# VectorE's order in the steady part written by hand, and one tensor-engine visit a tile for the local jobs

## The chip, the cores and the metric

The kernel runs on one core of a Trainium2 chip. The metric is the device time of one execution in microseconds (us). Five engines matter here, each with its own queue: TensorE (PE; its weight loads are PEld), VectorE (DVE), ScalarE (ACT), GpSimd (POOL) and SyncE (SP), which issues the DMAs.

## The reference

An attention layer feeds a feed-forward layer. There are 8 batches, 8 heads, 576 tokens and 64 channels a head; the feed-forward layer goes from 512 to 2048 and back to 512.

```python
scores = scale * q @ k.T                              # a head at a time
mask_local   = (rel >= 0) & (rel < 32)                # heads 0 to 3
mask_strided = (rel >= 0) & (pos_k % 32 == pos_q % 32)  # heads 4 to 7
attn = softmax(where(mask, scores, -1e9))
x = (attn @ v).transpose(0, 2, 1, 3).reshape(4608, 512)
h = x @ w_in                                          # 512 -> 2048
out = gelu(h) @ w_out                                 # 2048 -> 512
```

All of it is float32.

## The kernel before

**Tiles and steps.** The 4608 tokens make 12 tiles of 384 (`NTILE`, `TT`). The 2048 hidden channels make 16 chunks of 128 (`NF`), so the feed-forward layer has 192 steps; step n belongs to tile n // 16 and chunk n % 16, and `ready[t] = 16 t` is the first step of tile t. Every float32 operand is held as a high part and the difference to it, and a product is three matmuls. In a step, `ffn_h(n)` makes 12 matmuls (L602 to L604) into one of two PSUM banks with the tag H; `ffn_g(n)` lets ScalarE apply gelu in place (L611) and copy the high part gh (L613), and VectorE make the difference gl (L615); `ffn_o(n - 2)` makes 9 matmuls (L641 to L643) into three output banks. `store` copies a finished tile out.

**Attention.** The first four heads are local. A local job (`band_job`, 3 a tile, `JPT`) covers 128 tokens and yields between its parts: (0) score matmuls, L290, into the banks S0 and S1; (1) VectorE takes the masked minimum, L304; (2) ScalarE's exp, L308; (3) VectorE normalises and transposes, L311 to L314, and SyncE copies eight blocks into a band; (4) value matmuls, L328; (5) ScalarE's high part of x, L230; (6) VectorE's difference, L232. The other four heads are strided and run on VectorE alone but for their exp. A unit of up to 4 rows has `strided_qk`: a fill of the scores by GpSimd, one product-and-sum for each pair of rows (L477), a maximum and its subtraction (L485, L486); then `strided_av`: sum, reciprocal and quotient (L503 to L507), one multiply-add for each pair (L517, L519), and a transpose (L527, `fin`), which puts a `split` on a list: ScalarE's high part and VectorE's difference into the tile of x.

**Order.** The first 16 steps (`NB`) and the attention of the first two tiles are an order written out by hand (`START`), for all engines. The steady part is a loop over `step(n)`. Inside `tc.manual_schedule(engines=...)` the named engines run their instructions in the order in which the program issues them; the others are ordered by a scheduler, which may put a later instruction ahead of one that it believes is not ready. Before the change TensorE and ScalarE are named in the steady part, and VectorE, GpSimd and SyncE are scheduled.

**What a step issues, before.** `visit(n)`: at step 2 of a tile the score matmuls of the three local jobs of the next tile (`score_at`), at step 12 their value matmuls (`value_at`). Then H, gelu, gh and gl of step n; the high parts and differences of splits made earlier; `softmaxes(n)`, which issues parts 5, 6, 1, 2 and 3 of the local jobs; ScalarE's strided exps (`flush_exps`); a share of the strided list (`run_strided`); and the O matmuls of step n - 2. The share is set by sums of estimated costs:

```python
need = last[c] + (last[c + 1] - last[c]) * min(1.0, max(0.0, (n - a + 1) / (e - a - 3)))
run_strided(max(need, tot * (n - N0) / (ready[-1] - 3 - N0)))
```

Here c is the tile, a and e its first step and the next tile's (a is one more in tile 0), `last[t]` the summed cost up to the last entry that tile t needs, `tot` all of it. The list goes unit by unit: the q-k part of unit u, then the value part of unit u - 1.

Of the kernel before, what the change touches and what calls it, by code (L numbers as in the profile page):

```python
# [23 lines left out]
P = 128  # L24
STRIDE = 32
TT = 384
LU = 64
# [55 lines left out]
def attn_ffn_kernel(ctx: ExitStack, tc: tile.TileContext, qk, vl, qka, va, qs, ks, vs, w, out):  # L83
# [36 lines left out]
    def rows(j):  # L120
        return slice(j * D, (j + 1) * D)
# [112 lines left out]
    def local_job(x, banks=None, dve=0, pn=-1):  # L234
# [35 lines left out]
        dst = [a[:, 0:N2, c0:c0 + P] for a in x_tile(t)]  # L270
        yield from to_x(*dst, xv)

    def band_job(x, bt, sx=None):

        QB = STRIDE
        i = x % JPT if sx is not None else 0
        sx = {} if sx is None else sx
        if i == 0:  # L280
            sx["s"] = [ps_a.tile([P, DM], F32, name=f"S{j}_L{x}", tag=f"S{j}") for j in range(2)]
        s = [t[:, i * P:(i + 1) * P] for t in sx["s"]]
        qv = jq[x][:, 0:2 * N2 * LU].rearrange("p (r a t) -> p r a t", r=N2, a=2)
        kv = jq.pop(x)[:, 2 * N2 * LU:].rearrange("p (r a t) -> p r a t", r=N2, a=2)
        head = [(h % 2, slice(h // 2 * 2 * QB, (h // 2 + 1) * 2 * QB)) for h in range(HL)]
        for h in range(0, HL, 2):
            for g in range(P // QB):
                a, b = divmod(g, 2)
                for j in range(2):
                    nc.tensor.matmul(s[j][g * QB:(g + 1) * QB, head[h][1]],  # L290
                                     qv[rows(j), h // 2, a, b * QB:(b + 1) * QB],
                                     kv[rows(j), h // 2, a, b * QB:(b + 2) * QB],
                                     start=True, stop=True, tile_position=(j * D, g * QB))
        yield
        p1 = lpool.tile([P, 4 * LK], F32, name=f"P_L{x}", tag="P", bufs=2)
        p2 = lpool.tile([P, DM], F32, name=f"PT_L{x}", tag="PT", bufs=2)
        pb, pt = p2[:, 0:DM // 2], p2[:, DM // 2:]
        pv = pb.rearrange("p (c h t) -> p c h t", c=2, h=HL)
        nm, ss, rs = small(f"L{x}")
        first_ = [a for a in range(2) if LPLACE[2 * x + a][1] == 0]  # L300
        msk = bmask[first_[0] if first_ else None]
        for h in range(HL):
            j, cs = head[h]
            nc.vector.tensor_tensor_reduce(p1[:, h * 2 * QB:(h + 1) * 2 * QB], s[j][:, cs], msk, -SC, 3.0e38,  # L304
                                           ALU.add, ALU.min, nm[:, h:h + 1])
        yield
        for h in range(HL):
            nc.scalar.activation(pv[:, :, h, :], p1[:, h * 2 * QB:(h + 1) * 2 * QB].rearrange(  # L308
                "p (c t) -> p c t", c=2), AF.Exp, bias=nm[:, h:h + 1], scale=-1.0, accum_out=ss[:, h:h + 1])
        yield  # L310
        nc.vector.tensor_scalar_add(ss, ss, 1e-9)  # L311
        nc.vector.reciprocal(rs, ss)
        nc.vector.tensor_tensor(pv, pv, rs.unsqueeze(1).unsqueeze(3).to_broadcast([P, 2, HL, QB]), ALU.mult)
        nc.vector.transpose(pt, pb)  # L314
        tv = pt.rearrange("p (c q) -> p c q", c=2)
        for g in range(P // QB):
            for c in range(2):
                kb = g % 2 + c
                nc.sync.dma_start(bt[kb * QB:(kb + 1) * QB, g, :], tv[g * QB:(g + 1) * QB, c, :])
        yield  # L320
        if i % 2 == 0:
            sx["x"] = ps_a.tile([P, DM], F32, name=f"X_L{x}", tag="X" if i == 0 else "S0")
        xv = sx["x"][:, i % 2 * N2 * P:(i % 2 + 1) * N2 * P].rearrange("p (r q) -> p r q", r=N2)
        bv = bt.rearrange("p (a b) (h q) -> p a b h q", a=2, h=HL)
        for r in range(N2):
            for a in range(2):
                for j in range(2):
                    nc.tensor.matmul(xv[rows(j), r, a * LU:(a + 1) * LU], jv[x][:, a, 2 * r + j, :],  # L328
                                     bv[:LK, a, :, 2 * r + j, :], start=True, stop=True)
        jv.pop(x)  # L330
        load_jv(x + 3)
        yield
        t, c0 = divmod(x * P, TT)
        dst = [d[:, 0:N2, c0:c0 + P] for d in x_tile(t)]
        yield from to_x(*dst, xv)


    ka = {}
# [120 lines left out]
    def flush_exps(u):  # L459
        while exps and exps[0][0] <= u:  # L460
            exps.pop(0)[1]()

    def strided_qk(u):
        vi, _, r0, nr, t, k = PLACE[u]
        W = r0 + nr
        ops = []

        def init():
            s = spool.tile([P, UR, NR], F32, name=f"sc_{u}", tag="sc", bufs=3)[:, 0:nr]
            nc.gpsimd.memset(s[:, :, 0:W], NEG)  # L470
            ss[u] = s
        ops.append((0.0, init))
        for c in range(W):
            for r in range(max(0, c - r0), nr):
                def f(r=r, c=c):
                    junk = spool.tile([P, D], F32, name=f"junk_{u}_{r}_{c}", tag="junk", bufs=4)
                    nc.vector.tensor_tensor_reduce(  # L477
                        junk, sq[vi, "q"][:, r0 + r, :], sq[vi, "k"][:, c, :], 1.0, 0.0,
                        ALU.mult, ALU.add, ss[u][:, r, c:c + 1])
                ops.append((0.137, f))  # L480

        def sm():
            s = ss[u][:, :, 0:W]
            m = spool.tile([P, UR], F32, name=f"m_{u}", tag="m")[:, 0:nr]
            nc.vector.tensor_reduce(m, s, AX.X, ALU.max)  # L485
            nc.vector.tensor_tensor(s, s, m.unsqueeze(2).to_broadcast([P, nr, W]), ALU.subtract)  # L486
            exps.append((u, lambda: nc.scalar.activation(s, s, AF.Exp, scale=SC)))  # L487
        ops.append((0.25, sm))
        return ops
# [163 lines left out]
    strided = []  # L653
    N0 = 17
    U0 = sum(x[4] <= NA for x in PLACE)
    for u in range(U0, NU + 1):
        for v, what, names in ((u, strided_qk, "qk"), (u - 1, strided_av, "v")):
            if U0 <= v < NU:
                vi, _, r0, nr, t, _ = PLACE[v]
                strided += [(t, c, f) for c, f in what(v)]  # L660
                if r0 + nr == VISITS[vi][2] and vi in last_of:
                    strided.append((t, 0.0, lambda g=last_of[vi], ns=names: [load_strided(g, nm) for nm in ns]))
# [105 lines left out]

    SCORES, VALUES = 2, 12
    score_at = {ready[t - 1] + SCORES: t for t in range(2, NTILE)}
    value_at = {ready[t - 1] + VALUES: t for t in range(2, NTILE)}
    banks = {}
    local = {}
    band = slot("band", [P, 4 * DM])
    nc.gpsimd.memset(band, 0.0)
    NBT = 3
# [2 lines left out]
    def part(x, *which):  # L781

        for p in which:
            if p == 0:
                local[x] = [band_job(x, bts[x % NBT], banks), 0]
            assert local[x][1] == p
            local[x][1] += 1
            if next(local[x][0], True) is not None:
                load_jq(x + 3)

    def visit(n):

        for at, p in ((score_at, 0), (value_at, 4)):
            for i in range(JPT if n in at else 0):
                part(at[n] * JPT + i, p)

    def softmaxes(n):

        for i in range(JPT if n in value_at else 0):
            part(value_at[n] * JPT + i, 5, 6)  # L800
        for i in range(JPT if n in score_at else 0):
            part(score_at[n] * JPT + i, 1)
        for i in range(JPT):
            for d, p in ((1, 2), (2, 3)):
                t = score_at.get(n - 2 * i - d)
                if t is not None:
                    if p == 2:
                        flush_exps(NU)
                    part(t * JPT + i, p)

    def step(n):

# [2 lines left out]
        visit(n)  # L815
        if NB <= n < NS:
            ffn_h(n)
            for _ in ffn_g(n):
                pass
        old = len(splits)  # L820
        while old and n >= xfree[splits[0][0]]:
            for _ in splits.pop(0)[1]():
                pass
            old -= 1
        softmaxes(n)
        flush_exps(NU)
        if c + 1 < NTILE:
            a, e = ready[c] + (1 if c == 0 else 0), ready[c + 1]
            need = last[c] + (last[c + 1] - last[c]) * min(1.0, max(0.0, (n - a + 1) / (e - a - 3)))
            run_strided(max(need, tot * (n - N0) / (ready[-1] - 3 - N0)))  # L830
        if n == NS + 1:
            ffn_o(n - 3, n - 2)
        elif n >= NB + 2 and n < NS:
# [1 line left out]
        if n >= NB + 2 and (n - 2) % NF == NF - 1:  # L835
            store((n - 2) // NF)

    with tc.manual_schedule(engines={ET.Activation, ET.PE}):
        for n in range(NB, NS + 1):
            step(n)  # L840
    with tc.manual_schedule(engines={ET.Activation, ET.PE}):
        step(NS + 1)


# [63 lines left out]
```

## Time and profile before

| what | value |
| --- | --- |
| median of 3 runs | 885.21 us (884.99 to 885.87) |
| the profiled execution's own time | 885.1 us |
| its span in the profile | 883.2 us |
| TensorE clock granted, mean | 0.983 |
| TensorE busy | 858.5 us, 97% of the span |
| VectorE busy | 716.7 us, 81% |
| ScalarE busy | 492.7 us, 56% |

The span runs from the first to the last instruction of the profiled execution; the execution's own time has a little more around it. Busy times are of engines, not of the queues ahead of them. In the rows below, a group or an instruction has its line in the kernel, its engine, its operation and its tiles (out<-in); a number in brackets at the end is the idle time of the engine just before it, with what ended it.

### The profile page before, as it was taken

What the parts mean: (1) busy time and instruction counts of PE and PEld (TensorE: products, weight loads), DVE (VectorE), ACT (ScalarE), POOL (GpSimd) and SP (SyncE); (2) the same over time, 40 slices, a digit from 0 to 9 for tenths busy, and PEclk for the clock granted to TensorE, in tenths of its full rate; (3) what the DMA queues carried; (4) which work ended last, traced back from release to release, by engine and by line L of the source; (5) the groups of instructions that cost most, each with busy time, mean ns of one, the idle gap of its engine ahead of it and who ended that gap; (6) DMA issues with size and microseconds to landing.
All of it is one profiled execution on the core that took longest, in us unless ns stands there. A gap on an engine that the chain in (4) does not pass through costs nothing.

```text
span 883.2 us, 19381 instructions
## 1 busy us (share of the span) xinstructions
PE 858.5 (97%) x5984; PEld 769.2 (87%) x5984; DVE 716.7 (81%) x4897; ACT 492.7 (56%) x1003; POOL 17.9 (2%) x89
## 2 busy tenths in 40 slices
PE   4599999999999999999999999999999999999998
PEld 3488899989989889889898988998988998989997
DVE  5999999988898998898999978998789897752111
ACT  5999576358447347357636536636642743643222
POOL 5000100000000000000000000000000000000000
PEclk7599999999999999999999999999999999999999
DMA  9981420230220122112113022113012102000001
GB/s 304 348 350 56 149 82 15 86 102 23 85 81 14 62 69 77 36 42 75 58 32 109 18 75 82 21 55 127 17 57 82 49 25 63 11 11 1 36 1 36
DMA packets 34551, 66.66 MB, mean 75 GB/s; under 512 B 6800, under 2 KB 16528, under 8 KB 32400
## 3 DMA queue, kind: packets, MB, share of 16 engines
q1 hardware_dynamic: 34448, 65.43, 22.7%
q8 instruction: 47, 0.77, 0.4%
q14 instruction: 56, 0.46, 0.2%
HBM read 51.64 MB, written 9.44 MB: 69 GB/s over the span
## 4 chain that ended last, share of the span: by engine, by line
PE 93%; DVE 3%; DMA 2%; SPq 1%; issue 1%; ACT 1%; DVEq 0%
PE H L602 15%; PE O L642 15%; PE O L643 15%; PE H L604 15%; PE H L603 15%; PE O L641 15%; PE X_L L328 2%; DMA vl<-in_vl_dram 2%; PE S_L L290 1%; DVE ws L153 1%; DVE w L163 1%; DVE ws L155 1%; ACT ws L151 0%; SPq L132 0%; DVE xl L424 0%
## 5 line engine op out<-in xcount | busy, mean ns | idle before, releaser
L611 ACT ACTIVATE H<-H 128x384 f32<-128x384 f32 x192 | 91.5, 477 | 334.6 <-PE H L604 295.6
L602 PE MATMUL H<-xh,w 128*128 128x384 f32 x768 | 262.4, 342 | 2.6 <-ACT xh L230 1.2
L604 PE MATMUL H<-xh,w 128*128 128x384 f32 x768 | 260.3, 339 | 1.6 <-DVE w L163 1.6
L603 PE MATMUL H<-xl,w 128*128 128x384 f32 x768 | 259.2, 338 | 0.2 <-DVE xl L232 0.2
L519 DVE SCALAR_TENSOR_TENSOR acc<-sv,sc,acc 128x64 f32<-128x64 f32 x1158 | 250.2, 281 | 0.6
L643 PE MATMUL O<-w,gl 128*128 128x512 f32 x576 | 227.9, 396 | 0.0
L642 PE MATMUL O<-w,gh 128*128 128x512 f32 x576 | 227.5, 395 | 0.0
L641 PE MATMUL O<-w,gh 128*128 128x512 f32 x576 | 224.2, 389 | 0.0
L477 DVE CUSTOM_DVE_ANT_0 junk<-sq,sk 128x64 f32<-128x64 f32 x1290 | 206.2, 221 | 1.8 <-DMA sk<-in_ks_dram 1.8
L615 DVE TENSOR_TENSOR gl<-H,gh 128x384 fp32r<-128x384 f32 x192 | 106.3, 554 | 107.8 <-ACT gh L613 107.4
L602 PEld LDWEIGHTS H<-xh,w 128*128 128x128 f32 x768 | 145.2, 189 | 12.5 <-ACT xh L230 1.4
L603 PEld LDWEIGHTS H<-xl,w 128*128 128x128 f32 x768 | 145.1, 189 | 7.9 <-DVE xl L232 0.6
L604 PEld LDWEIGHTS H<-xh,w 128*128 128x128 f32 x768 | 145.0, 189 | 2.0 <-DVE w L163 1.9
L643 PEld LDWEIGHTS O<-w,gl 128*128 128x128 f32 x576 | 108.0, 187 | 23.0
L642 PEld LDWEIGHTS O<-w,gh 128*128 128x128 f32 x576 | 108.0, 187 | 18.2
L641 PEld LDWEIGHTS O<-w,gh 128*128 128x128 f32 x576 | 108.2, 188 | 17.4
L477 DVE DVE_READ_ACCUMULATOR2_ANT sc<- 128x1 f32 x1290 | 109.3, 85 | 0.0
L613 ACT CAST gh<-H 128x384 fp32r<-128x384 f32 x192 | 92.3, 481 | 6.0
L611 ACT ACT_TABLE_LOAD x61 | 78.3, 1283 | 1.1
L487 ACT ACT_TABLE_LOAD x35 | 44.9, 1283 | 0.6
L308 ACT ACTIVATE PT_L<-P_L,nm_L 128x64 f32<-128x64 f32 x132 | 44.3, 336 | 0.3
L308 ACT ACT_TABLE_LOAD x25 | 32.1, 1283 | 2.7 <-DMA band<-PT_L 2.2
(106 smaller groups left out, 512.0 us busy)
## 6 DMA issues: line engine op xcount, KB each, us to landing
ws<-in_w_dram SPq DMA_DIRECT2D x16, 1024.0 KB, 11.4
qk<-in_qk_dram SPq DMA_DIRECT2D x36, 320.0 KB, 4.7
out_dram<-ob SPq DMA_DIRECT2D x34, 256.0 KB, 2.5
vl<-in_vl_dram SPq DMA_DIRECT2D x36, 192.0 KB, 3.4
sk<-in_ks_dram SPq DMA_DIRECT2D x8, 576.0 KB, 4.9
sv<-in_vs_dram SPq DMA_DIRECT2D x8, 576.0 KB, 3.7
band<-PT_L SPq DMA_DIRECT2D x240, 16.0 KB, 1.8
sq<-in_qs_dram SPq DMA_DIRECT2D x4, 576.0 KB, 3.8
```

What stands on the lines that cost most here:

```text
L308: nc.scalar.activation(pv[:, :, h, :], p1[:, h * 2 * QB:(h + 1) * 2 * QB].rearrange("p (c t) -> p c t", c=2), AF.Exp, bias=nm[:, h:h + 1], ...
L477: nc.vector.tensor_tensor_reduce(junk, sq[vi, "q"][:, r0 + r, :], sq[vi, "k"][:, c, :], 1.0, 0.0, ALU.mult, ALU.add, ss[u][:, r, c:c + 1])
L519: nc.vector.scalar_tensor_tensor(acc[:, r, :], sq[vi, "v"][:, c, :], wgt, acc[:, r, :], ALU.mult, ALU.add)
L602: nc.tensor.matmul(hp, w1[f][:, 0, c, :], xh[:, c, :], start=(c == 0), stop=False)
L603: nc.tensor.matmul(hp, w1[f][:, 0, c, :], xl[:, c, :], start=False, stop=False)
L604: nc.tensor.matmul(hp, w1[f][:, 1, c, :], xh[:, c, :], start=False, stop=(c == NC - 1))
L611: nc.scalar.activation(hp, hp, AF.Gelu)
L613: nc.scalar.copy(gh, hp)
L615: nc.vector.tensor_tensor(gl, hp, gh.bitcast(F32), ALU.subtract)
L641: nc.tensor.matmul(o, gh[:, sl], w2[f][:, 0, :], start=(f == 0), stop=False)
L642: nc.tensor.matmul(o, gh[:, sl], w2[f][:, 1, :], start=False, stop=False)
L643: nc.tensor.matmul(o, gl[:, sl], w2[f][:, 0, :], start=False, stop=(f == NF - 1))
```

## The change

1. VectorE joins TensorE and ScalarE in `manual_schedule` for the steady part.
2. The last VectorE instruction of `ffn_g(n)` (gl) and of the splits taken in step n is kept in a list `later` and issued at the head of step n + 1. The differences of x of the local jobs are issued one step after their high parts as well.
3. `visit(n)` makes the value matmuls of tile t and the score matmuls of tile t + 1 at one step, step 12 of a tile. The scores of tile 2 keep a visit of their own (step 18), and the last value visit has no scores. The value results of the third job go into the unused last columns of the next tile's two score banks.
4. Parts 1, 2 and 3 of the local jobs are spread over the steps behind: job i has them 1, 2 and 3 steps after the visit plus 4 i (2 i for tile 2). Part 3 stands behind the step's strided work. The next q-k load of the local jobs is issued right behind the score matmuls.
5. The strided list goes with the value part two units behind the q-k part instead of one; it is to be done one step earlier (4 instead of 3); the scores have 4 buffers instead of 3.

The core of the diff:

```diff
+        if i == 0:
+            sx["x"] = ps_a.tile([P, DM], F32, name=f"X_L{x}", tag="X")
+        xv = [sx["x"][:, (2 * r + i) * P:(2 * r + i + 1) * P] if i < 2 else sx[x // JPT + 1][r][:, JPT * P:]
+              for r in range(N2)]
...
-            s = spool.tile([P, UR, NR], F32, name=f"sc_{u}", tag="sc", bufs=3)[:, 0:nr]
+            s = spool.tile([P, UR, NR], F32, name=f"sc_{u}", tag="sc", bufs=4)[:, 0:nr]
...
-    for u in range(U0, NU + 1):
-        for v, what, names in ((u, strided_qk, "qk"), (u - 1, strided_av, "v")):
+    for u in range(U0, NU + 2):
+        for v, what, names in ((u, strided_qk, "qk"), (u - 2, strided_av, "v")):
...
+    FIRST, VISIT = 2, 12
+    value_at = {ready[t - 1] + VISIT: t for t in range(2, NTILE)}
+    score_at = {ready[1] + FIRST: 2, **{n: t + 1 for n, t in value_at.items()}}
+    soft_at = {}
+    for n, t in score_at.items():
+        for i in range(JPT):
+            for p in (1, 2, 3):
+                soft_at.setdefault(n + p + i * (2 if t == 2 else 4), []).append((t * JPT + i, p))
...
     def step(n):
         c = n // NF
         visit(n)
         if NB <= n < NS:
             ffn_h(n)
-            for _ in ffn_g(n):
-                pass
+        for p in later:
+            next(p, None)
+        later.clear()
+        if n - 1 in value_at:
+            for i in range(2):
+                part(value_at[n - 1] * JPT + i, 6)
+        if n - 2 in value_at:
+            part(value_at[n - 2] * JPT + 2, 6)
+        if NB <= n < NS:
+            g = ffn_g(n)
+            next(g), next(g)
+            later.append(g)
         old = len(splits)
         while old and n >= xfree[splits[0][0]]:
-            for _ in splits.pop(0)[1]():
-                pass
+            g = splits.pop(0)[1]()
+            next(g)
+            later.append(g)
             old -= 1
-        softmaxes(n)
+        if n in value_at:
+            for i in range(2):
+                part(value_at[n] * JPT + i, 5)
+        if n - 1 in value_at:
+            part(value_at[n - 1] * JPT + 2, 5)
+        soft = [(x, p) for x, p in soft_at.get(n, ()) if x < NJ]
+        for x, p in soft:
+            if p < 3:
+                part(x, p)
         flush_exps(NU)
         if c + 1 < NTILE:
...
-            need = last[c] + (last[c + 1] - last[c]) * min(1.0, max(0.0, (n - a + 1) / (e - a - 3)))
-            run_strided(max(need, tot * (n - N0) / (ready[-1] - 3 - N0)))
+            need = last[c] + (last[c + 1] - last[c]) * min(1.0, max(0.0, (n - a + 1) / (e - a - 4)))
+            run_strided(max(need, tot * (n - N0) / (ready[-1] - 4 - N0)))
+        for x, p in soft:
+            if p == 3:
+                part(x, p)
...
-    with tc.manual_schedule(engines={ET.Activation, ET.PE}):
+    with tc.manual_schedule(engines={ET.DVE, ET.Activation, ET.PE}):
         for n in range(NB, NS + 1):
             step(n)
```

More of the change, by code (lines that the diff above doesn't have):

```diff
@@ L271, in local_job, with score_banks @@
         yield from to_x(*dst, xv)
+    def score_banks(t):
+        return [ps_a.tile([P, DM], F32, name=f"S{j}_{t}", tag=f"S{j}") for j in range(2)]
     def band_job(x, bt, sx=None):
@@ L278, in band_job @@
         i = x % JPT if sx is not None else 0
[L279 to L282, printed above, removed]
+        sx = {x // JPT: score_banks(x // JPT), "alone": True} if sx is None else sx
+        s = [t[:, i * P:(i + 1) * P] for t in sx[x // JPT]]
         qv = jq[x][:, 0:2 * N2 * LU].rearrange("p (r a t) -> p r a t", r=N2, a=2)
@@ L320, in band_job @@
         yield
-        if i % 2 == 0:
-            sx["x"] = ps_a.tile([P, DM], F32, name=f"X_L{x}", tag="X" if i == 0 else "S0")
-        xv = sx["x"][:, i % 2 * N2 * P:(i % 2 + 1) * N2 * P].rearrange("p (r q) -> p r q", r=N2)
+        if i == 0:
+            sx["x"] = ps_a.tile([P, DM], F32, name=f"X_L{x}", tag="X")
+        xv = [sx["x"][:, (2 * r + i) * P:(2 * r + i + 1) * P] if i < 2 else sx[x // JPT + 1][r][:, JPT * P:]
+              for r in range(N2)]
         bv = bt.rearrange("p (a b) (h q) -> p a b h q", a=2, h=HL)
@@ L327, in band_job @@
                 for j in range(2):
-                    nc.tensor.matmul(xv[rows(j), r, a * LU:(a + 1) * LU], jv[x][:, a, 2 * r + j, :],
+                    nc.tensor.matmul(xv[r][rows(j), a * LU:(a + 1) * LU], jv[x][:, a, 2 * r + j, :],
                                      bv[:LK, a, :, 2 * r + j, :], start=True, stop=True)
@@ L333, in band_job @@
         t, c0 = divmod(x * P, TT)
-        dst = [d[:, 0:N2, c0:c0 + P] for d in x_tile(t)]
-        yield from to_x(*dst, xv)
+        two = sx["x"].rearrange("p (r w) -> p r w", r=N2)
+        if i == 2:
+            both = [(xv[r], (r, slice(c0, c0 + P))) for r in range(N2)]
+        elif "alone" in sx:
+            both = [(two[:, :, 0:P], (slice(0, N2), slice(c0, c0 + P)))]
+        else:
+            both = [(two, (slice(0, N2), slice(0, 2 * P)))] if i else []
+        parts = [to_x(*[w_[(slice(None),) + d] for w_ in x_tile(t)], src) for src, d in both]
+        for p in parts:
+            next(p)
+        yield
+        for p in parts:
+            next(p, None)
     ka = {}
@@ L767, in attn_ffn_kernel @@
         load_strided(order_g[1], nm)
-    SCORES, VALUES = 2, 12
-    score_at = {ready[t - 1] + SCORES: t for t in range(2, NTILE)}
-    value_at = {ready[t - 1] + VALUES: t for t in range(2, NTILE)}
+    FIRST, VISIT = 2, 12
[6 more added lines that the diff above has]
+                soft_at.setdefault(n + p + i * (2 if t == 2 else 4), []).append((t * JPT + i, p))
     banks = {}
-    local = {}
+    local, later = {}, []
     band = slot("band", [P, 4 * DM])
@@ L787, in part @@
             local[x][1] += 1
-            if next(local[x][0], True) is not None:
+            next(local[x][0], None)
+            if p == 0:
                 load_jq(x + 3)
     def visit(n):
[L793 to L809, printed above, removed]
+        t = value_at.get(n, 0)
+        if n in score_at:
+            banks[score_at[n]] = score_banks(score_at[n])
+        for i in range(JPT if t else 0):
+            part(t * JPT + i, 4)
+        for i in range(JPT if score_at.get(n, NTILE) < NTILE else 0):
+            part(score_at[n] * JPT + i, 0)
     def step(n):
@@ L817, in step @@
             ffn_h(n)
-            for _ in ffn_g(n):
-                pass
+        for p in later:
+            next(p, None)
+        later.clear()
[8 more added lines that the diff above has]
+            later.append(g)
         old = len(splits)
         while old and n >= xfree[splits[0][0]]:
-            for _ in splits.pop(0)[1]():
-                pass
+            g = splits.pop(0)[1]()
+            next(g)
+            later.append(g)
             old -= 1
-        softmaxes(n)
+        if n in value_at:
[7 more added lines that the diff above has]
+                part(x, p)
         flush_exps(NU)
@@ L836, in step @@
             store((n - 2) // NF)
-    with tc.manual_schedule(engines={ET.Activation, ET.PE}):
+    with tc.manual_schedule(engines={ET.DVE, ET.Activation, ET.PE}):
         for n in range(NB, NS + 1):
             step(n)
-    with tc.manual_schedule(engines={ET.Activation, ET.PE}):
+    with tc.manual_schedule(engines={ET.DVE, ET.Activation, ET.PE}):
         step(NS + 1)
```

## The prediction

> **What bounds the kernel now.** I read the page first: the busy shares, the forty slices and the chain that ended last.
>
> ```profile
> span 883.2 us, 19381 instructions
> PE 858.5 (97%) x5984; PEld 769.2 (87%) x5984; DVE 716.7 (81%) x4897; ACT 492.7 (56%) x1003; POOL 17.9 (2%) x89
> ...
> PEclk7599999999999999999999999999999999999999
> ...
> PE 93%; DVE 3%; DMA 2%; SPq 1%; issue 1%; ACT 1%; DVEq 0%
> ```
>
> TensorE is busy 97% of the span at full clock behind the start, and 93% of the chain runs through it. Then busy time in two stretches, one of steps 16 to 27 and one of a whole later tile (us, then PE, PEld, DVE, ACT, POOL):
>
> ```profile
> 107.00:162.00 55.00, 55.00 (x408) 49.59 (x407) 51.53 (x463) 34.97 (x71) 0.40 (x3) 1.00 0.15 48
> 303.00:373.00 70.00, 70.00 (x482) 63.00 (x481) 61.44 (x456) 36.70 (x79) 0.35 (x3) 1.00 0.19 57
> ```
>
> TensorE has no idle time in either. So in the steady part only two things can move the end: less work on TensorE, or a stall that is not there now. But VectorE is 94% busy in the first stretch (51.53 of 55) and 88% in the second. It has little to give there, and the change takes from it the freedom to choose what runs next. From the view of waits, two pairs:
>
> ```profile
> PEld H L602 <- DVE gl L615: 0.6, 2, 0.5
> ...
> DVE z L503 <- ACT sc L487: 18.0, 21, 1.1
> ```
>
> The first is the wait that matters: H of a step waits for a gl. The H banks are two, and step n+2 can't write its bank before gl(n), the last reader, is done. Here that cost 0.6 us in all.
>
> **Part 1: TensorE visits.** The matmuls in order of time, around a score visit (step 2 of a tile, L290) and a value visit (L328):
>
> ```profile
> 181.82 0.33 PE L602 MATMUL H<-xh,w 128*128 128x384 f32 x1
> ...
> 185.77 0.40 PE L643 MATMUL O<-w,gl 128*128 128x512 f32 x1
> 186.10 1.17 PE L290 MATMUL S_L<-qk 64*32 64x64 f32 x96
> 187.20 0.45 PE L602 MATMUL H<-xh,w 128*128 128x384 f32 x1
> 187.48 0.34 PE L603 MATMUL H<-xl,w 128*128 128x384 f32 x1
> ...
> 191.50 0.33 PE L602 MATMUL H<-xh,w 128*128 128x384 f32 x1
> ...
> 195.68 0.33 PE L602 MATMUL H<-xh,w 128*128 128x384 f32 x1
> ...
> 228.95 0.40 PE L643 MATMUL O<-w,gl 128*128 128x512 f32 x1
> 229.27 1.62 PE L328 MATMUL X_L<-band,vl 96*64 96x64 f32 x48
> 230.82 0.44 PE L602 MATMUL H<-xh,w 128*128 128x384 f32 x1
> ```
>
> A plain step is 195.68 - 191.50 = 4.18 us. The step that ends with the score visit has 187.20 - 181.82 = 5.38, and the H behind it is 0.11 late once more (its first two matmuls start 0.28 apart, against 0.17 in plain steps): 1.31 us in all. The value visit, by the same sum (230.82 - 228.95 less the 0.23 of an ordinary start, plus 0.11), is 1.75 us. The matmuls of a visit stay as many. What a visit costs beside them is the entry (186.10 - 185.77 = 0.33, against 0.23: 0.10) and the exit (0.11 for the first matmul and about 0.11 for the last small ones): 0.32 us.
>
> Merging nine of the ten score visits with value visits removes nine entries and nine exits, but puts a change from L328 to L290 inside. The start part shows one:
>
> ```profile
> 53.39 1.01 PE L328 MATMUL X_L<-first,vl 96*64 96x64 f32 x16
> 54.34 0.46 PE L290 MATMUL S_L<-qk 64*32 64x64 f32 x32
> ```
>
> Sixteen L328 take 0.95 us there; at the pitch of the 48-matmul visit (1.55 / 48 = 0.032) they would take 0.52, so the change costs between nothing and 0.43. The nearer bound is the exit that every visit pays, 0.11 to 0.14. I take 0.13, and the gain is 0.32 - 0.13 = 0.19 a merge, **1.7 us for nine** (0 to 2.9 by the ends). [...]
>
> **Part 2: VectorE by hand.** Now every instruction waits for the one ahead of it in the written order: gl(n-1) stands behind all of step n-1's strided products. The counts below are from the kernel's own lists; the durations are from these rows in order of time:
>
> ```profile
> 402.02 0.22 DVE L477 CUSTOM_DVE_ANT_0 junk<-sq,sk 128x64 f32<-128x64 f32 x1
> ...
> 402.17 0.22 DVE L477 CUSTOM_DVE_ANT_0 junk<-sq,sk 128x64 f32<-128x64 f32 x1
> ...
> 402.46 0.56 DVE L615 TENSOR_TENSOR gl<-H,gh 128x384 fp32r<-128x384 f32 x1
> 402.93 0.22 DVE L477 CUSTOM_DVE_ANT_0 junk<-sq,sk 128x64 f32<-128x64 f32 x1
> ...
> 405.81 0.21 DVE L485 TENSOR_REDUCE m<-sc 128x4 f32<-128x56 f32 x1
> ...
> 406.19 0.55 DVE L615 TENSOR_TENSOR gl<-H,gh 128x384 fp32r<-128x384 f32 x1
> ...
> 407.92 0.23 DVE L304 CUSTOM_DVE_ANT_0 P_L<-S_L,bmaskNone 128x64 f32<-128x64 f32 x1 [0.97 <-ACT PT_L L308]
> ...
> 408.50 0.17 DVE L311 TENSOR_SCALAR ss_L<-ss_L 128x4 f32<-128x4 f32 x1
> ...
> 409.53 0.45 DVE L314 STREAM_TRANSPOSE PT_L<-PT_L 128x256 f32<-128x256 f32 x1
> ...
> 411.74 0.17 DVE L503 TENSOR_REDUCE z<-sc 128x2 f32<-128x12 f32 x1 [0.97 <-ACT sc L487]
> ...
> 412.55 0.42 DVE L517 TENSOR_SCALAR acc<-sv,sc 128x64 f32<-128x64 f32 x2
> ...
> 414.89 0.31 DVE L527 STREAM_TRANSPOSE xs<-acc 128x128 f32<-128x128 f32 x1
> ...
> 474.57 3.41 DVE L519 SCALAR_TENSOR_TENSOR acc<-sv,sc,acc 128x64 f32<-128x64 f32 x17
> ```
>
> A q-k product comes every 0.146, a weighted v every 0.2 (3.41 / 17), a gl takes 0.47, a masked minimum of four heads 0.58 (407.92 to 408.50), a local softmax's normalising chain 1.48 (408.50 to 409.98), the strided maximum and its subtraction about 0.47, the sum-to-quotient chain 0.81. The last three are chains in which each waits for the one before. The scheduler now puts other work into their gaps; the hand order runs them unbroken.
>
> The binding place is the tile of steps 16 to 31, since the strided work due there grows: the list now also runs a unit further ahead (35 more q-k products before the last av), and has 12 steps instead of 13. Steps 17 to 25 issue 147 q-k (21.5 us), 44 weighted v (8.8), 9 gl (4.2), 3 masked minima (1.7), 3 normalisings (4.4), 4 maxima (1.9), 3 quotient chains (2.4), 2 transposes and one x difference (1.3, at up to half as much again as the 0.31 row): 46.2 us. gl(25), at the head of step 26, adds 0.5. The chain starts with gl(16):
>
> ```profile
> 113.88 0.56 DVE L615 TENSOR_TENSOR gl<-H,gh 128x384 fp32r<-128x384 f32 x1 [0.29 <-ACT gh L613]
> ...
> 154.38 0.22 DVE L485 TENSOR_REDUCE m<-sc 128x4 f32<-128x64 f32 x1
> ...
> 113.91 0.34 PE L602 MATMUL H<-xh,w 128*128 128x384 f32 x1
> ...
> 154.95 0.33 PE L602 MATMUL H<-xh,w 128*128 128x384 f32 x1
> ...
> 116.70 0.48 ACT L613 CAST gh<-H 128x384 fp32r<-128x384 f32 x1
> ```
>
> 113.88 + 46.7 = 160.6, where H(27) would start at 154.95 and needs it: **5.6 us of stall**, spread over steps 24 to 27. I take 5.3, as a chain or two may find its inputs sooner. The 154.38 row agrees: even now the 16-row unit's maximum, listed in step 25 (its H two steps before 154.95, at 146.6), runs only then. VectorE is late already; what saves TensorE is that gl goes past the queue.
>
> For the two tiles behind, the same count gives 55.0 us for steps 32 to 43 and 55.2 for 48 to 59, against 12 x 4.18 = 50.2. The cover is the second H bank: gh(17) is ready 3.3 us after H(17) starts (113.91, 116.70 + 0.48), gl ends 0.5 later, and it is needed 8.4 after: 4.5 us. So 4.8 overruns by 0.3, and 5.0 with the 0.4 left over from the step before by 0.9. Later tiles ask for 47 to 51 us in their first twelve steps: no stall. **Stalls: 5.3 + 0.3 + 0.9 = 6.5 us** (0 to 9.4: all waits covered, or every duration 2.5% longer).
>
> [...]
>
> **What is moved and costs nothing.** The x differences move a step back: a unit's transpose falls by step e-5, its cast in e-4, its difference in e-3, three steps (12.5 us) before H of tile e reads it; less the 4.5 us of lag it still holds. The eight band copies of a local job (SyncE) leave at the end of a step, the last job's five steps before the visit that reads them. The q-k loads are issued at the score visit instead of behind the last difference, 16 steps before use. VectorE's 18.0 us behind ScalarE's strided exp (L503 above) go, as av runs two units behind; that only refills what the hand order idles. GpSimd's fills have a fourth buffer. The clock I cost at nothing: the slices show it lower only in the start, where TensorE was idle half the time, and the stalls here are at most 2 us in a step of 4.2.
>
> **Sum.** The profiled execution took 885.1 us (883.2 of span and 1.9 around it), 0.1 below the median. -1.7 + 6.5 = +4.8 on 885.1: **889.9**, and as much for the median.
>
> **Rivals.** (a) VectorE keeps up, and only the merge is left: faster. It is decided in steps 17 to 25 of the first tile: if their work takes under 41 us from gl(16) on (113.88 to 154.95) instead of 46.2, H(27) finds its bank free. The saturated 94% and the late 154.38 row speak against it; for it speaks that products listed early may run in the start part's gaps. 885.2 - 1.7 = 883.5. (b) The chains' gaps cost nothing: 0.6 a normalising, 0.25 a quotient chain, 0.2 a maximum less, 3.3 us in steps 17 to 25. Then 2.0 us of stall in the first tile, none behind: +0.3, 885.5, no change. (c) ScalarE, which waits for VectorE's maxima and transposes in its own order, hands the lag back: gelu late, gh late. The price of 2.5% more on every row stands for it: 9.4 - 1.7, 892.9.
>
> **Chances.** Forecast (stall of 4 to 8 us, 887.5 to 891.5) 0.5; (a) 0.17; (b) with all between 0.2; (c) 0.13. The range takes in (a) to (c): 883.2 to 893; the likeliest case's own is 887.5 to 891.5. A measurement of this kernel tells some 0.2% (1.8 us) from no change: faster 0.17, same 0.2, slower 0.63.
>
> **What would show it.** Right: TensorE idle before the first matmul of H in the first tile, at 140 to 162 us, released by VectorE's gl, five us in all, and an us or so near 225 to 300; merged visits of about 2.9 us, at eleven places instead of twenty. Wrong: no wait of H for gl (then a), a VectorE chain of normalising under 1 us (then b), or ScalarE named before H (then c). The forecast falls if the written order isn't kept on VectorE, or if the banks of H were freed by something before gl.

## The result: slower by 8.6 us, and the profile after

The changed kernel takes 893.7 us (median of 4 runs, 893.45 to 894.0) against 885.13 (884.99 to 885.87): a ratio of 1.0096, 95% interval 1.0082 to 1.011. Slower was forecast, and by 4.8 us; the time lies 0.7 above the range. The profiled execution's span went from 883.2 to 891.5 us. The page after, its busy shares and chain:

```profile
span 891.5 us, 19417 instructions
PE 861.2 (97%) x5984; PEld 766.2 (86%) x5984; DVE 732.8 (82%) x4897; ACT 497.9 (56%) x1007; POOL 17.8 (2%) x89
...
PEclk9999999999999999999999999999999999999999
...
PE 71%; DVE 19%; DMA 6%; issue 2%; ACT 2%; SPq 1%; DVEq 0%; ACTq 0%
```

VectorE was on 3% of the chain that ended last and is now on 19%. The view of waits over the whole run (us in total, times, longest):

```profile
DVE gl L629 <- ACT gh L627: 88.1, 35, 3.6
...
DVE P_L L305 <- ACT xh L230: 28.6, 9, 3.5
...
PEld H L616 <- DVE gl L629: 15.3, 21, 2.1
PE H L616 <- DVE gl L629: 7.1, 10, 1.7
```

The last two were 0.6 and 0.3 us before. They are the stall that the prediction names: TensorE at the head of a step, H waiting for gl. The second row is new, and the prediction doesn't have it: VectorE waits nine times, about 3.2 us each, for ScalarE's high part of x before it may take a masked minimum. The same view over steps 61 to 171 alone (312 to 800 us), where no stall was forecast:

```profile
DVE P_L L305 <- ACT xh L230: 22.4, 7, 3.5
...
PEld H L616 <- DVE gl L629: 7.4, 11, 1.9
...
PE H L616 <- DVE gl L629: 3.2, 5, 1.5
```

And busy time in three stretches (us, then PE, PEld, DVE, ACT, POOL), the first two as shown of before:

```profile
107.00:162.00 55.00, 51.83 (x348) 45.58 (x347) 50.80 (x456) 37.73 (x74) 0.24 (x2) 1.00 0.20 65
303.00:373.00 70.00, 70.00 (x484) 63.14 (x483) 62.73 (x481) 39.28 (x82) 0.50 (x4) 1.00 0.20 66
373.00:443.00 70.00, 69.31 (x479) 62.30 (x478) 62.71 (x481) 41.55 (x84) 0.56 (x4) 1.00 0.15 49
```

TensorE, which had no idle time in the first stretch, loses 3.2 us of 55 there, and 0.7 in the third, which begins in step 75.

**Where the 8.6 us are.** From the starts of H of each step in both traces (H of step 191 starts 8.2 us later than before):

| term | forecast | measured |
| --- | --- | --- |
| nine merged visits | -1.7 | -1.9 |
| stalls, tile of steps 16 to 31 | +5.3 | +5.1 (4.2, and 0.9 at the visit of step 28) |
| stalls, the two tiles behind | +0.3, +0.9 | +0.6, +0.9 |
| stalls, tiles from step 80 on | 0 | +6.0 |
| plain steps, 4.187 to 4.174 us, some 173 of them | 0 | -2.3 |
| start part | 0 | -0.14 |
| sum | +4.8 | +8.3 |

The measured terms are good to about 0.1 us; the expectations below have 5.2 where the table has 5.1. The 8.6 is between medians, and the two profiled executions are 8.3 apart. Two terms were not in the forecast at all. The experiments go after them first.

**The place of the new wait.** TensorE's merged visit of one later tile and the steps behind it, in order of time (start, us, instruction, [idle before]):

```profile
374.42 1.15 PE L331 MATMUL X_L<-band,vl 96*64 96x64 f32 x32
375.40 0.64 PE L331 MATMUL S<-band,vl 96*64 96x64 f32 x16
375.96 1.17 PE L291 MATMUL S<-qk 64*32 64x64 f32 x96
377.06 0.44 PE L616 MATMUL H<-xh,w 128*128 128x384 f32 x1
```

ScalarE and VectorE beside it, from the same view:

```profile
379.96 0.48 ACT L627 CAST gh<-H 128x384 fp32r<-128x384 f32 x1
...
380.47 0.56 DVE L629 TENSOR_TENSOR gl<-H,gh 128x384 fp32r<-128x384 f32 x1 [2.34 <-ACT gh L627]
380.96 0.69 DVE L232 TENSOR_TENSOR xl<-X_L,xh 128x512 fp32r<-128x512 f32 x1
...
383.77 0.47 ACT L625 ACTIVATE H<-H 128x384 f32<-128x384 f32 x1
384.28 0.48 ACT L627 CAST gh<-H 128x384 fp32r<-128x384 f32 x1
384.65 0.44 ACT L230 CAST xh<-S 128x128 fp32r<-128x128 f32 x2
384.96 0.23 DVE L305 CUSTOM_DVE_ANT_0 P_L<-S,bmaskNone 128x64 f32<-128x64 f32 x1 [3.30 <-ACT xh L230]
```

The scores were done at 377. But the third job's values lie in the last columns of the same two banks S, and the program issues ScalarE's copy of them (L230, 384.65) ahead of VectorE's read of the scores (L305). That copy is issued behind gelu and gh of the next step, so VectorE, with a written order and nothing that may go past, stands from 381.66 to 384.96 with the step's strided products queued behind. It catches up only over the rest of the tile. Both instructions only read the bank, and different columns of it. This trace shows that the one waits for the other, and the price, 28.6 us in nine waits; why it must wait, no run here shows.

### The profile page after: what moved, and what is told of

It is laid out like the page before. It is cut to its first block, busy times and chain, and to the rows that moved or that the text cites. A ratio compares the mean times of both kernels' runs of the same rounds, so it can differ in the third digit from the quotient of the medians.

```text
span 891.5 us, 19417 instructions
## 1 busy us (share of the span) xinstructions
PE 861.2 (97%) x5984; PEld 766.2 (86%) x5984; DVE 732.8 (82%) x4897; ACT 497.9 (56%) x1007; POOL 17.8 (2%) x89
## 4 chain that ended last, share of the span: by engine, by line
PE 71%; DVE 19%; DMA 6%; issue 2%; ACT 2%; SPq 1%; DVEq 0%; ACTq 0%
PE H L616 12%; PE H L618 11%; PE H L617 11%; PE O L657 11%; PE O L656 11%; PE O L655 11%; DVE acc L533 6%; DVE junk L491 5%; DMA ws<-in_w_dram 3%; DVE gl L629 2%; PE X_L L331 1%; PE S L291 1%; DMA sq<-in_qs_dram 1%; DMA qk<-in_qk_dram 1%; DVE acc L531 1%
## 5 line engine op out<-in xcount | busy, mean ns | idle before, releaser
L533 DVE SCALAR_TENSOR_TENSOR acc<-sv,sc,acc 128x64 f32<-128x64 f32 x1158 | 239.7, 282 | 1.1
L491 DVE CUSTOM_DVE_ANT_0 junk<-sq,sk 128x64 f32<-128x64 f32 x1290 | 194.5, 220 | 0.0
L491 DVE DVE_READ_ACCUMULATOR2_ANT sc<- 128x1 f32 x1290 | 106.8, 83 | 0.0
```

The source lines that it names most:

```text
L491: nc.vector.tensor_tensor_reduce(junk, sq[vi, "q"][:, r0 + r, :], sq[vi, "k"][:, c, :], 1.0, 0.0, ALU.mult, ALU.add, ss[u][:, r, c:c + 1])
L533: nc.vector.scalar_tensor_tensor(acc[:, r, :], sq[vi, "v"][:, c, :], wgt, acc[:, r, :], ALU.mult, ALU.add)
```

## The experiments

Theory from here on: (A) the bank wait makes the stalls of the later tiles; (B) in the first tile it is the amount of VectorE's work before step 28 (12 steps, the value part two units behind); (C) the fourth score buffer changes the plain step by where it puts tiles in memory.

### The local softmax one step later

```diff
-                soft_at.setdefault(n + p + i * (2 if t == 2 else 4), []).append((t * JPT + i, p))
+                soft_at.setdefault(n + p + (t > 2) + i * (2 if t == 2 else 4), []).append((t * JPT + i, p))
```

> The changed kernel, but from tile 3 on the local jobs' masked minimum, exp and normalising come one step later, so that the minimum of the first job no longer stands right behind the step in which ScalarE copies the third job's values out of the same bank. Theory (bank wait): the changed kernel's VectorE waits 28.6 us in 9 places for that copy, once a tile, and the lag it leaves costs TensorE the 6.0 us of stalls in tiles 5 to 10; without it those stalls go and about 887.7 us come out, with 6 to 7 us of stalls left in the tiles of steps 16 to 63. Rival (VectorE has too much work in every tile): the wait only moves to the next gh, the stalls stay, 893 to 894 us.

Measured: 889.17 us (888.32 to 889.35), ratio to before 1.0038 (1.0025 to 1.0051), 4.5 below the changed kernel. Its waits over 312 to 800 us, in order of size; the 22.4 of L305 stood between these two and is gone, and no row names H on TensorE:

```profile
DVE gl L629 <- ACT gh L627: 24.1, 22, 3.3
ACT H L625 <- DVE sc L491: 16.9, 6, 3.2
```

Nothing else was moved, and the stalls from step 64 on are gone: 6.0 us become 0.1. A is shown. The two tiles before that lose 2.3 us instead of 1.5, so that H of step 191 starts 5.1 us sooner and not 6.0; the median is 1.5 above the 887.7 that was expected. The stall of the first tile stays at some 4.1 and 0.9, as B has it.

### VectorE left to the scheduler, all else as changed

```diff
-    with tc.manual_schedule(engines={ET.DVE, ET.Activation, ET.PE}):
+    with tc.manual_schedule(engines={ET.Activation, ET.PE}):
```

> The changed kernel with VectorE left to the scheduler, all else as changed (merged visits, longer list, differences a step later). Theory (the written order alone stalls TensorE): 12.7 us of stalls go, the merge's 1.9 us and the shorter pitch of the matmuls stay: 881 us, under the 885.1 of the kernel before. Rival (the longer list and the later differences stall whatever the order): 888 us or more.

Measured: 895.34 us (895.11 to 895.93), ratio 1.0107 (1.0093 to 1.0121). A miss: taking the hand order away alone does not bring the time back. The stalls from step 64 on fall from 6.0 to 0.6 us, and VectorE's wait for ScalarE's copy is not in the view of waits any more: there the written order is a part of the cause. But in the first tile 3.1 us are lost at H, and at the merged visit of step 28 TensorE waits for the copies of the third job's band. TensorE in order of time:

```profile
171.15 1.39 PE L331 MATMUL S<-band,vl 96*64 96x64 f32 x16 [7.78 <-DMA band<-PT_L]
172.48 1.62 PE L291 MATMUL S<-qk 64*32 64x64 f32 x96
...
174.51 0.52 PE L617 MATMUL H<-xl,w 128*128 128x384 f32 x1
174.83 0.52 PE L618 MATMUL H<-xh,w 128*128 128x384 f32 x1
...
176.04 0.34 PE L616 MATMUL H<-xh,w 128*128 128x384 f32 x1
176.22 0.34 PE L617 MATMUL H<-xl,w 128*128 128x384 f32 x1
```

and VectorE's normalising of that job:

```profile
154.93 0.17 DVE L312 TENSOR_SCALAR ss_L<-ss_L 128x4 f32<-128x4 f32 x1 [0.95 <-ACT PT_L L309]
158.92 0.17 DVE L313 RECIPROCAL rs_L<-ss_L 128x4 f32<-128x4 f32 x1
160.76 0.42 DVE L314 TENSOR_TENSOR PT_L<-PT_L,rs_L 128x256 f32<-128x256 f32 x1
162.72 0.44 DVE L315 STREAM_TRANSPOSE PT_L<-PT_L 128x256 f32<-128x256 f32 x1
```

Four dependent operations take 8.2 us, since strided work and gl stand in the gaps between them. The copies can leave only at 163.2, when the visit's first value matmuls are already running, and SyncE puts two strided loads between them:

```profile
165.06 0.53 SPq L468 DMA_DIRECT2D sq<-in_qs_dram  x1
165.63 0.43 SPq L468 DMA_DIRECT2D sk<-in_ks_dram  x1
166.10 3.09 SPq L320 DMA_DIRECT2D band<-PT_L  x5
```

So in this tile VectorE has not enough room in either order: the hand order is late with gl, the scheduler's with the band. The written order alone is not the cause there. That leaves the amount of work, B, which the next run tries.

### The value part one unit behind and thirteen steps, as before

```diff
-    for u in range(U0, NU + 2):
-        for v, what, names in ((u, strided_qk, "qk"), (u - 2, strided_av, "v")):
+    for u in range(U0, NU + 1):
+        for v, what, names in ((u, strided_qk, "qk"), (u - 1, strided_av, "v")):
...
-            need = ... (n - a + 1) / (e - a - 4)
-            run_strided(... (ready[-1] - 4 - N0))
+            need = ... (n - a + 1) / (e - a - 3)
+            run_strided(... (ready[-1] - 3 - N0))
```

> The changed kernel in hand order, but the strided list with the value part one unit behind, as before, and 13 steps for a tile's share instead of 12. Theory (work brought forward): the stall of steps 24 to 28, 5.2 us now, falls to about 1, since 35 products less are due in the first tile and 1 step more is there; the stalls of tiles 2 and 3 go too, those of tiles 5 to 10 behind the bank wait stay: 888 us. Rival (the chains' gaps alone): the stall of the first tile stays above 4 us, 892 us or more.

Measured: 886.78 us (886.48 to 887.28), ratio 1.001 (0.9999 to 1.002). The first tile stalls 0.8 us instead of 5.2. Its waits, down to H:

```profile
DVE P_L L305 <- ACT xh L230: 30.3, 9, 3.6
...
PEld H L616 <- DVE gl L629: 7.9, 16, 1.0
```

The bank wait is untouched, and some 5 us of stalls are left in the tiles behind: 1.2 around step 48, where none was expected, and 4.2 from step 64 on. For the first tile B is shown, the two edits taken as one; A and B are separate terms.

### The two together

> The changed kernel with the two edits of the last runs together: local softmax parts one step later from tile 3 on, and the strided list one unit behind with 13 steps for a tile's share. Theory (two separate causes that add up): the first tile's stall is about 0.9 us and tile 5 to 10's none, so 12.7 us of stalls become 1 to 2, and 882.0 to 883.2 us come out, under the kernel before. Rival (work that is taken from one place shows up at the next): the stalls do not add up, 885 us or more.

Measured: 881.77 us (881.47 to 881.86), ratio 0.996 (0.9946 to 0.9974): 3.4 us faster than the kernel before, 11.9 faster than the changed one. The busy shares of the page, then the busy time of the first stretch:

```profile
PE 857.0 (97%) x5984; PEld 768.3 (87%) x5984; DVE 733.7 (83%) x4897; ACT 490.3 (56%) x1001; POOL 17.8 (2%) x89
```

```profile
107.00:162.00 55.00, 54.76 (x442) 48.86 (x444) 47.92 (x394) 37.86 (x73) 0.24 (x2) 1.00 0.15 48
```

VectorE is as busy over the span as in the changed kernel (733.7 against 732.8); in this stretch it does 2.9 us less, and TensorE loses 0.2 instead of 3.2. Stalls left: 0.8 us in the first tile, 0.1 behind. What makes it faster than the kernel before is the merge (1.7 to 1.9 us) and a shorter plain step (2.3 us, taken up below), less 0.9 of stalls. No run shows a gain from VectorE's written order itself, and the merge with VectorE scheduled and these two edits in place was not run. The expectations below call this kernel x5.

### Which half of the second edit: two units behind, thirteen steps

```diff
-            need = ... (n - a + 1) / (e - a - 4)
-            run_strided(... (ready[-1] - 4 - N0))
+            need = ... (n - a + 1) / (e - a - 3)
+            run_strided(... (ready[-1] - 3 - N0))
```

with the softmax one step later.

> x5, but with the value part two units behind as in the change, 13 steps kept. It tells apart what brings the first tile's stall: by my count of the list the 12 steps make the larger part (5.9 against 1.5 us with 13 steps and two units, 0.9 with 13 and one). So about 1.5 us in the first tile here, 0.6 above x5. If the unit that is run ahead is the cause instead, 4 us of the stall stay, 3 us above x5.

Measured: 882.6 us (882.38 to 883.1), ratio 0.9971 (0.996 to 0.9982): 0.8 above the two together, with 1.8 us of stall in the first tile against 0.8. The step less was the larger part: with two units behind, 12 steps cost 5.1 us there and 13 cost 1.8.

### gl in the middle of its own step

The changed kernel, with gl(n) issued behind half of step n's strided share and not at the head of step n + 1:

```diff
-            run_strided(max(need, tot * (n - N0) / (ready[-1] - 4 - N0)))
+            upto = max(need, tot * (n - N0) / (ready[-1] - 4 - N0))
+            done = cum[pos[0] - 1] if pos[0] else 0.0
+            run_strided(done + (upto - done) / 2)
+            if n < NS:
+                next(later.pop(0), None)
+            run_strided(upto)
```

> The changed kernel, but gl of step n stands in the middle of step n's strided share instead of at the head of step n + 1. Theory (TensorE stalls because gl, which frees the H bank, stands behind all of a step's strided work): gl comes about 1.9 us sooner against the bank's next use wherever VectorE is late, so the first tile's stall falls from 5.2 to about 3.3, those of tiles 2 and 3 go, and those of tiles 5 to 10 fall from 6.0 to 1 or 2: 886 us. Rival (the amount of work on VectorE, not the place of gl): gl in the middle waits for gh and holds up what is behind it, the stalls stay, 892 us or more.

Measured: 893.7 us (893.09 to 894.76), ratio 1.0097 (1.0083 to 1.0111), the changed kernel's own time. The forecast of the time missed, but the theory holds in a part of the kernel. From step 64 on the stalls fall from 6.0 to 0.6 us, as it said. In the first tile the stall before H is 2.7 us, but the visit of step 28 adds 4.5, and the step behind it 1.0. The two tiles after that lose 3.5 us instead of 1.5. The waits of 117 to 172 us name H and the visit:

```profile
PE S L331 <- DMA band<-PT_L: 3.6, 2, 2.1
PEld H L616 <- DVE gl L629: 3.4, 4, 1.1
```

The 1.0 behind the visit is the clock (busy times, then the granted clock behind POOL's):

```profile
164.40:167.85 3.45, 1.13 (x49) 0.96 (x50) 3.45 (x17) 0.00 (x0) 0.00 (x0) 1.00 0.24 77
167.85:171.26 3.41, 3.41 (x94) 3.24 (x72) 1.41 (x6) 0.00 (x0) 0.11 (x1) 0.50 0.79 220
```

So in the later tiles the place of gl is a part of the cause: the bank wait is still there (17.3 us in nine places, against 28.6), but gl no longer stands behind all of a lagging step's work. In the first tiles, where VectorE has more work than the steps have time, what TensorE gains at H it pays at the visit and in the tiles behind.

### The plain step: the fourth score buffer in the kernel before

```diff
-            s = spool.tile([P, UR, NR], F32, name=f"sc_{u}", tag="sc", bufs=3)[:, 0:nr]
+            s = spool.tile([P, UR, NR], F32, name=f"sc_{u}", tag="sc", bufs=4)[:, 0:nr]
```

> The kernel before with 4 buffers of strided scores instead of 3, nothing else: it moves what is allocated behind them in the SBUF. In the changed kernel a plain step of 21 matmuls takes 4.174 us, in the kernel before 4.187, from the start part on, where the order is the same. Theory (places in the SBUF): the step falls to 4.174 us here as well, 882.8 us. Rival (the order of the other engines' work, or another chip): 4.187 and 885.1 us.

Measured: 886.2 us (885.65 to 886.91), ratio 1.0005 (0.9997 to 1.0014). SBUF names the memory in which these tiles lie. The time missed, the mechanism held: the plain step is 4.174 us, as in the changed kernel, but the scheduler, given one more buffer, made another order on VectorE with 3.7 us of stalls that were not there.

### The plain step again, under a written order

The two together with `bufs=3` (x7), and then that with an unused tile of the same size in the same pool:

```diff
-            s = spool.tile([P, UR, NR], F32, name=f"sc_{u}", tag="sc", bufs=4)[:, 0:nr]
+            s = spool.tile([P, UR, NR], F32, name=f"sc_{u}", tag="sc", bufs=3)[:, 0:nr]
...
+    pad = spool.tile([P, UR, NR], F32, name="pad", tag="pad", bufs=1)
+    nc.gpsimd.memset(pad, 0.0)
```

> x5 with 3 buffers of strided scores instead of 4; the order of all but GpSimd's fills is the same. Theory (places in the SBUF): the plain step goes back from 4.174 to 4.187 us, 2.3 us over 176 steps, and the time is 2.3 us above x5. Rival (the step's length comes from elsewhere): 4.174 and the time of x5.

> x7 (3 buffers of strided scores, plain step 4.187 us) with a tile of the same size that is filled once and never used, in the pool of the scores. Theory (places in the SBUF of what is allocated behind): the plain step is 4.174 us again, about 2.3 us under x7, near x5's 881.8. Rival (the fourth buffer itself, by letting GpSimd's fills run elsewhere): 4.187 us.

Measured: 885.16 us (883.67 to 885.8), ratio 0.9998 (0.9989 to 1.0006), without the tile; 881.73 (881.57 to 882.93), ratio 0.9966 (0.9954 to 0.9979), with it. Two H starts a step apart, first without the tile, then with it:

```profile
836.06 0.33 PE L616 MATMUL H<-xh,w 128*128 128x384 f32 x1
...
840.25 0.33 PE L616 MATMUL H<-xh,w 128*128 128x384 f32 x1
```

```profile
838.36 0.34 PE L616 MATMUL H<-xh,w 128*128 128x384 f32 x1
...
842.53 0.34 PE L616 MATMUL H<-xh,w 128*128 128x384 f32 x1
```

4.19 and 4.17, and 4.187 and 4.174 over many steps. A tile that nothing reads gives the step back, so it is where the tiles lie and not the buffer's use: C is shown. By 13 ns on 173 steps it is 2.3 us; the profiled executions without and with the tile are 1.9 apart, the medians 3.4, and what the other part of the medians' difference is stays open. So does which tiles' places matter. With three buffers the two together have the median of the kernel before.

### The merge alone: two visits again

The two together, with the scores at a visit of their own one step after the values:

```diff
-    score_at = {ready[1] + FIRST: 2, **{n: t + 1 for n, t in value_at.items()}}
+    score_at = {ready[1] + FIRST: 2, **{n + 1: t + 1 for n, t in value_at.items()}}
```

(the banks made at the value visit, and the softmax's steps left where they are).

> x5 with the score matmuls at a visit of their own, one step behind the values; all softmax parts stand at the same steps as in x5. It prices the merge alone. Theory: nine more entries and exits at 0.21 us each, 1.9 us, so 883.7 us. Rival (the change between the two kinds of small matmuls costs as much as leaving): the time of x5, 881.8.

Measured: 883.31 us (883.07 to 883.91), ratio 0.9982 (0.9973 to 0.9991), 1.5 above the two together. From H of step 16 to H of step 191 it takes 759.43 us against 757.71. With the late H behind it, a value visit costs 1.74 and a score visit 1.29, 3.03 together, and the merged one 2.84: 0.19 a merge, 1.7 us for nine.

## Why the prediction was right and where it was wrong

**Part 1 stands.** -1.7 forecast, -1.9 between the two kernels' traces, 1.7 with the merge undone alone. In the rows above the change from L331 to L291 inside a visit costs little: 375.40 to 375.96 is 0.56 for 16 matmuls, against the 0.52 of their plain pitch.

**Part 2, the first tiles: right in size and place, not in each step.** 6.5 us forecast for the three tiles, 6.6 measured. The stall of the first tile, as TensorE shows it in the changed kernel, with gl(25) on VectorE between:

```profile
152.73 0.44 PE L616 MATMUL H<-xh,w 128*128 128x384 f32 x1
...
158.27 0.52 DVE L629 TENSOR_TENSOR gl<-H,gh 128x384 fp32r<-128x384 f32 x1
158.85 0.44 PE L616 MATMUL H<-xh,w 128*128 128x384 f32 x1 [1.67 <-DVE gl L629]
...
165.07 0.57 PE L331 MATMUL S<-band,vl 96*64 96x64 f32 x12 [0.59 <-DMA band<-PT_L]
```

gl(25) ends at 158.8, where the count had 160.6. Of these 1.8 us, 1.0 is the start of the chain: gl(16) starts at 112.87 here, and the prediction took 113.88 from the trace of before. Only 0.8 (under 2%) is the work: 45.9 us from gl(16) to the end of gl(25), against 46.7, and the numbers of products, chains and gl are those that the prediction counted. H(27) starts 3.9 us later than before, and not 5.6; with the earlier start and the shorter plain step taken out, the stall by then is 4.2. Then comes 0.9 at the merged visit, of which 0.6 is a wait for the third job's band that the prediction costed at nothing. The agreement of 5.1 with 5.3 is in part two errors that cancel. The normalising chain does cost its full time in a written order, so rival (b) is out:

```profile
135.73 0.16 DVE L312 TENSOR_SCALAR ss_L<-ss_L 128x4 f32<-128x4 f32 x1
...
136.66 0.45 DVE L315 STREAM_TRANSPOSE PT_L<-PT_L 128x256 f32<-128x256 f32 x1
```

1.38 us from first start to last end, with nothing between the four operations; the prediction took 1.48.

**The step that failed: "Later tiles ask for 47 to 51 us in their first twelve steps: no stall."** The sentence takes VectorE's work for the only thing that delays it; with the same work and the softmax a step later there is no stall there. The change makes a wait: the scores now lie in a bank with values that ScalarE copies first (28.6 us of waits in nine places), and the copy stands behind gelu and gh of the next step. The prediction had the new place of the third job's values in the diff before it and never asked who reads that bank next, nor what stands behind the reader. Some 3.2 us of idle in a tile whose margin is 50.2 less 47 to 51 leaves a stall in six of the seven tiles from step 64 on: 6.0 us, all but 0.1 of them gone when the softmax moves one step. The written order and the place of gl have a share in it, since with the scheduler, or with gl in the middle of its step, 0.6 of the 6.0 is left.

More than half of the 6.0, 3.3 us, falls in the tile of steps 160 to 175, where VectorE, late from the bank wait, also waits for a load of strided values. The first line is that wait in the changed kernel; the second is from the view of waits of the run with the softmax one step later:

```profile
778.20 0.74 DVE L531 TENSOR_SCALAR acc<-sv,sc 128x64 f32<-128x64 f32 x4 [3.21 <-DMA sv<-in_vs_dram]
```

```profile
DVE acc L531 <- DMA sv<-in_vs_dram: 3.3, 1, 3.3
```

There the same load is waited for as long and TensorE loses nothing. So the load alone is within the margin, and with the bank wait ahead of it it is not.

**A second term, of the other sign: the fourth buffer.** "GpSimd's fills have a fourth buffer" was costed at nothing. As a buffer it is worth nothing that these runs show: an unused tile in its stead shortens each plain step as much, from 4.187 to 4.174 us, 2.3 us in all. The prediction shows no row of before that tells it. The two misses, +6.0 and -2.3, make 3.7 of the 3.8 by which the forecast was short.

**The rivals.** (a), VectorE keeps up, is what the two edits together nearly give (1 us of stall left), and not what the change as it stood did. (c) had the nearest number, 892.9, by a mechanism that turned out the other way round: VectorE waits for ScalarE. ScalarE's gelu does wait for VectorE's strided products (16.9 us in six places from 312 to 800 us), but it does so as long in the run with the softmax one step later, where no stall is left there. The clock, costed at nothing, has a 9 (90% or more) in every slice of the page after. In the page of before the first two slices have 7 and 5, and yet H of step 16 starts only 0.14 us later there.

## What to carry to other kernels

When an engine gets a written order, a count of its work is only half of the sum: follow every new wait of that engine too, and ask what stands in line behind it and how much slack the stage has left. Two results in one PSUM bank tied their readers together here, for 28.6 us in nine waits; where results share a bank, look for the engine that reads first and what is issued ahead of that read. When a step changes its length by a fixed few nanoseconds (13 here) with the same instructions, try an unused tile before looking for a cause in the order.

## What the runs showed of the hardware

- The same 21 matmuls of a step, in the same order, take 4.187 us with three score buffers, and 4.174 with four or with three and an unused tile of the same size.
- One stall by itself, of up to 2.1 us in front of a step, left the clock as it was: behind 1.67 us at 157.2 in the changed kernel the granted clock is 1.00, and behind 2.08 us at 150.7 in the run with the scheduler's order O's matmuls stand 0.23 us apart from 155.00 on, as in plain steps. Two close together did not: in the run with gl in the middle of its step TensorE idles 1.51 and 2.10 us at the visit, is busy 1.13 of the 3.45 us up to 167.85, and is granted 0.50 from there to 171.26; H's matmuls stand 0.32 us apart from 169.66 to 171.26, and 0.17 behind it. In the scheduler's run, behind the wait of 7.8 us that ends at 171.15, H's matmuls stand 0.32 us apart from 174.51 to 175.8, and 0.17 from 176.04 on.
